# Refitted task durations in the list scheduler of a windowed attention and softplus feed-forward kernel

## Chip, cores and metric

One core of a Trainium2 chip. The metric is the device time of one execution in microseconds, the median of three runs.

## The reference

Windowed attention over 8 batches, 8 heads, 576 positions and 64 columns per head, then a feed-forward part with softplus on the 4608 tokens it gives. All in float32.

```python
scores = scale * np.matmul(q, k.transpose(0, 1, 3, 2))
mask_plain = (rel >= 0) & (rel < 32)                        # heads 0 to 3
mask_dil = (rel >= 0) & (rel < 128) & (rel % 4 == 0)        # heads 4 to 7
scores = np.where(masks, scores, -1e9)
attn = np.exp(scores - np.max(scores, axis=-1, keepdims=True))
attn = attn / (np.sum(attn, axis=-1, keepdims=True) + 1e-09)
x = np.matmul(attn, v)            # then 4608 tokens x 512
h = x @ w_in                      # 512 x 2048
g = np.maximum(h, 0.0) + np.log1p(np.exp(-np.abs(h)))
out = g @ w_out                   # 2048 x 512
```

## The kernel before, in words

The 4608 tokens are 9 chunks of 512. Attention of a chunk is 4 groups, one for each pair of heads, so there are 36 groups, `groups[0]` to `groups[35]`. For a group TensorE makes two visits, both of small matmuls: the scores (64 of them, `score_of`, tile `sv_ps<-k,q`) and, later, the values (64 of them, `value_of`, tile `sv_ps<-pt,v`). Between the two lies a chain: VectorE scales and masks the scores (L441) and takes the maximum (L452), ScalarE computes 8 exponentials (L463), VectorE the divisor (L475, L478), the division (L481) and a transpose of 32 x 32 squares (L503), and two DMAs through DRAM turn the squares (`turned`, then `pt`). The values of group n - 1 and the scores of group n use the two halves of the same banks.

The feed-forward part works on weights and activations that are split into a high and a low part, so a product is three wide matmuls (128 x 128 by 128 x 512). Chunks 0 to 2 go in 48 slots (`h_part`, `o_part`, softplus in between). Chunks 3 to 8 go as three doubles of two chunks; each double multiplies 2 x 2 blocks by seven products in place of eight: `product` (tiles `h_x`, `h_y`) for `w_in`, with an `aside` that takes every product out of its bank (L1424 on ScalarE, L1426 on VectorE), a late softplus unit of three ScalarE operations (L1437, L1440, L1443) and one VectorE operation (L1447) on 128 x 1024, sums of blocks (L1462), a high part on ScalarE and a low part on VectorE (L1467, L1471), and then `block_step` (tile `o_ps`) for `w_out`.

Two things order the work. Up to slot 22 (`HANDED`) the order is a written list (`OPENING`) and a loop that spreads VectorE's work over the slots. After that a list scheduler plans the rest: each piece of work is a `Task` with an engine, a cost in microseconds, tasks that it depends on, and a rank. The scheduler runs a clock; when an engine is free in the plan it emits the open task of the lowest rank on VectorE, ScalarE, GpSimd (POOL) and SyncE (SP, which issues the DMAs), and for TensorE chooses between three queues: `first` (h and products), `second` (o and block steps) and `visits`. Emission order is the order on each engine's queue on the chip; nothing is reordered there, and each instruction waits for the semaphores of what it needs. So a planned time has no force on the chip: only the order has.

`Task.open` is the test of whether a task may begin, `run` books an engine's time and the task's end, `values_of` and `attention` make the tasks of attention. `choose` takes the scores of group n when they are open and `joins` says that the values of group n - 1 can go with them (then both are emitted as one visit), or when they are overdue, or when neither other queue is open. `joins` asks that the turned squares landed at least `MARGIN` ago in the plan. At least 8 us (`VISIT_EVERY`) pass between visits. DMAs have a planned rate and landing time, `RATE` and `LANDING`.

Of the kernel before, what the change touches and what calls it, by code (L numbers as in the profile page):

```python
# [66 lines left out]
VALUED = 14.6, 17.1, 19.8  # L67
URGENT = -20.0
HANDED_VISIT = 2.0
MARGIN = 0.4  # L70
VISIT_EVERY = 8.0
NEG = -1.0e9
DEPTH = 4
# [43 lines left out]
def tile_windowed_attention_softplus_ffn(  # L117
# [804 lines left out]
    def score_of(n):  # L922
        shared[n] = two_banks("sv_ps")
        groups[n].score(shared[n])
# [91 lines left out]
    assert not events  # L1016

    MM, LATENCY, RATE, LANDING = 0.227, 0.06, 0.32, 2.3
    SHARED, FROM_PSUM = 1.0, ("aside", "put", "scaled", "max", "turn", "resumed", "finished", "plus 2", "plus 3", "plus 4")
    DVE, ACT, POOL, SP, PE = "DVE", "ACT", "POOL", "SP", "PE"  # L1020
    steps = (
# [9 lines left out]
    class Ring:  # L1031
# [7 lines left out]
        def take(self, until):  # L1039
            self.holders = self.holders[1:] + [until]  # L1040

    class Task:

        serial = itertools.count()
# [13 lines left out]
        def open(self, t):  # L1058
            return (
                self.after <= t + 1e-9  # L1060
                and all(
                    d.over(t + LATENCY * (getattr(d, "engine", PE) == self.engine != PE)) for d in self.deps
                )
                and all(ring.open(t) for ring, _ in self.takes)
                and (self.engine != SP or self.rank < 2.0 or arrived[0] <= t)
            )
# [28 lines left out]
    free_at = dict.fromkeys((PE, *queues), 0.0)  # L1095
# [8 lines left out]
    def run(task, t, engine=PE):  # L1104
        for ring, until in task.takes:
            ring.take(until)
        task.emit()
        cost = task.cost
        if engine == DVE and cost > 0.40 and not task.name.startswith(FROM_PSUM):
            cost += min(max(free_at[POOL] - t, 0.0), SHARED)  # L1110
        if task.engine == SP:
            free_at[SP] = t + 0.08
            task.end = arrival(t, task.cost)
        else:
            free_at[task.engine] = t + cost
            task.end = t + cost + LATENCY + 0.2 * (task.engine == PE)
        heapq.heappush(ends, task.end)
        heapq.heappush(ends, free_at[task.engine])
        if engine in queues:
            queues[engine].remove(task)  # L1120
# [172 lines left out]
    def values_of(n):  # L1293

        deps = [brought.get(n), loaded.get((n, "v")), scaled_of.get(n + 1), x_done.get(n - 1)]
        v = valued[n] = Task(f"values {n}", PE, 1.30, lambda: value_of(n), deps)
        if n + 1 < len(groups):
            loaded[n + 1, "v"] = Task(f"v {n + 1}", SP, 0.512, groups[n + 1].load_v, [v], rank=1.0)
        x_done[n] = Task(
            f"x {n}", ACT, 0.60, groups[n].x_high, [v, scaled_of.get(n + 1), *x_uses.get(n // 2, [])], rank=0.3  # L1300
        )

    def attention(n):

        soon[0] = SOONER
        if n == len(groups):
            values_of(n - 1)
            return
        g = groups[n]
        deps = [scaled_of.get(n - 1), x_done.get(n - 2), loaded[n, "k"], loaded[n, "q"]]  # L1310
        s = scored[n] = Task(f"scores {n}", PE, 1.06, lambda: score_of(n), deps)
        scaled = scaled_of[n] = Task(
            f"scaled {n}", DVE, 0.69, g.maximum, [s, turned_of.get(n - 1), masks_in.get(g.c)], rank=0.25
        )
        last = Task(f"max {n}", DVE, 0.69, g.greatest, [scaled], rank=0.26)
        loads(n + 1)
        values_of(n - 1)
        for t in range(NB):
            last = Task(
                f"exps {n} {t}", ACT, 0.34, lambda t=t: g.exponentials(slice(t, t + 1)), [last], rank=0.3 + 0.01 * t  # L1320
            )
        last = Task(f"divisor {n}", DVE, 0.40, g.divisor, [last], rank=0.3)
        last = Task(f"divide {n}", DVE, 0.70, lambda: g.divide(nc.vector), [last], rank=0.3)
        last = turned_of[n] = Task(f"turn {n}", DVE, 0.71, g.turn_squares, [last, sent_squares.get(n - 1)], rank=0.3)
        last = sent_squares[n] = Task(f"send {n}", SP, 0.256, g.send_squares, [last], rank=0.1)
        brought[n] = Task(f"bring {n}", SP, 0.5, g.fetch_squares, [last, valued[n - 1]], rank=0.1)
# [203 lines left out]
    for d in range(DOUBLES):  # L1530
        for p in range(NPAIR):
            for k, (x, weights, role, begins, to, temp) in enumerate(steps):
                b = (role + p) % 2
                task = Task(
                    f"product {d} {p} {k}", PE, 6 * MM,
                    lambda d=d, p=p, w=weights, x=x, b=b, s=begins: product(d, p, w, x, b, s),
                )
                n = len(steps) * p + k
                base = given + 2 * len(in_turn) * d
                if d == 0:  # L1540
                    task.upto = min(base, given - 2 * NKT + n)
                else:
                    task.upto = base - SPILL + min(n, SPILL)
                task.upto += due(d, n)
                product_done[d, p, x] = product_done[d, p, weights] = task
                at_n = len(steps) * (NPAIR * d + p) + k
                task.deps.append(asides.get(at_n - 2) or plus_done[46 + k])
                first.append(task)
                c = p // 2
                if isinstance(to, int):  # L1550
                    emit = lambda to=to, b=b, temp=temp: aside(temps(to), b, temp)
                else:
                    emit = lambda p=p, to=to, b=b, temp=temp: aside(raw_g(p // 2, *to)[:, p % 2], b, temp)
                mine = asides[at_n] = Task(
                    f"aside {d} {p} {k}", ACT if temp is None else DVE, 0.62 if temp is None else 0.70,
                    emit, [task, before],
                )
                before = mine
                if isinstance(to, int):
                    if d == 0 and p == 0:  # L1560
                        mine.deps.append(Later(lambda: written.get(NPAIR - 1)))
                    continue
                if d and p % 2 == 0:
                    users = {(0, 0): "s2", (0, 1): "s4", (1, 0): "s3", (1, 1): "s1"}
                    mine.deps.append(block_done[d - 1, users[to], c])
                    if to == (1, 1):
                        mine.deps.append(combined[d - 1, "s2", c])
                    if to == (0, 0):
                        mine.deps.append(combined[d - 1, "s4", c])
                elif d == 0 and p % 2 == 0:  # L1570
                    tag = 4 * c - 3 + {(0, 0): 0, (1, 1): 1, (1, 0): 2, (0, 1): 3}[to]
                    if c or to == (0, 1):
                        if tag % 2 == 0 or tag // 2 < RESIDENT:
                            mine.deps += [product_done[0, tag // 2, w] for w in (("b21",), ("b22", "t4"))[tag % 2]]
                        mine.deps.append(
                            Later(lambda q=tag // 2: two_kept.get(q)) if tag % 2 else kept_one[tag // 2]
                        )
                    else:
                        mine.deps.append(out_free[16 + tag])
                if p % 2 == 0:  # L1580
                    unit_first[to] = mine
                    continue
                key = c, *to
                name = f"{d} {key}"
                n = softened
                softened += 1
                plus = unit_done[d, key] = Task(f"plus {name}", DVE, 1.24, lambda key=key: late_softplus(key))
                takes = [(e_ring, plus)]
                one = Task(f"abs {name}", ACT, 1.16, lambda n=n, key=key: abs_of(n, key), [mine, unit_first[to], last_abs[0]], takes=takes)
                last_abs[0] = one  # L1590
                two = Task(f"exp {name}", ACT, 1.16, lambda key=key: late_exp(key), [one])
                plus.deps.append(Task(f"log {name}", ACT, 1.16, lambda key=key: late_log(key), [two]))
                if n == 1:
                    one.deps.append(Later(lambda: two_kept.get(6)))
        for turn, (i, c) in enumerate(in_turn):
# [167 lines left out]
    for n in range(double, len(groups)):  # L1763

        def both(n=n):
            score_of(n)
            value_of(n - 1)

        together[scored[n]] = Task(f"both {n}", PE, 2.10, both)
    spaced, done_second = HANDED_VISIT, 0  # L1770

    def joins(v, t):
# [219 lines left out]
```

## Time and profile before

| what | us |
|---|---|
| median of 3 runs | 831.25 (829.7 to 832.61) |
| the profiled execution's own time | 833.33 |
| its span, first to last instruction | 831.5 |
| TensorE busy | 815.6 |
| VectorE busy | 656.1 |
| ScalarE busy | 577.7 |
| GpSimd busy | 64.0 |

The granted TensorE clock was 0.989 over the span, and 1.00 in every slice after the first 50 us. A busy TensorE is not TensorE at its pace: matmuls are pipelined and their ends are modelled, so the starts of groups of matmuls are what to compare. In the rows below PE is TensorE, PEld its weight load, DVE VectorE, ACT ScalarE, POOL GpSimd and SP SyncE; L12 is line 12 of the kernel, and `out<-in` are the program's tile names.

### The profile page before, as it was taken

What the parts mean: (1) busy time and instruction counts of PE and PEld (TensorE: products, weight loads), DVE (VectorE), ACT (ScalarE), POOL (GpSimd) and SP (SyncE); (2) the same over time, 40 slices, a digit from 0 to 9 for tenths busy, and PEclk for the clock granted to TensorE, in tenths of its full rate; (3) what the DMA queues carried; (4) which work ended last, traced back from release to release, by engine and by line L of the source; (5) the groups of instructions that cost most, each with busy time, mean ns of one, the idle gap of its engine ahead of it and who ended that gap; (6) DMA issues with size and microseconds to landing.
All of it is one profiled execution on the core that took longest, in us unless ns stands there. A gap on an engine that the chain in (4) does not pass through costs nothing.

```text
span 831.5 us, 19565 instructions
## 1 busy us (share of the span) xinstructions
PE 815.6 (98%) x7841; PEld 662.6 (80%) x7841; DVE 656.1 (79%) x935; ACT 577.7 (69%) x1241; POOL 64.0 (8%) x74
## 2 busy tenths in 40 slices
PE   6899999999999999999999999999999999999997
PEld 3688888888888888788888888788878888888786
DVE  5798899957897798678889986778798957577964
ACT  6797778857676877578889546786796436776632
POOL 0000000031353360000000000000000000000000
PEclk7899999999999999999999999999999999999999
DMA  8788944468999887665777769897867576667662
GB/s 249 249 273 267 308 132 144 135 205 264 300 318 340 308 317 236 208 201 187 219 228 238 259 198 309 271 279 255 269 222 235 175 242 215 185 194 215 215 200 105
DMA packets 99947, 194.82 MB, mean 234 GB/s; under 512 B 10128, under 2 KB 43024, under 8 KB 99856
## 3 DMA queue, kind: packets, MB, share of 16 engines
q1 hardware_dynamic: 99712, 193.29, 72.1%
q8 instruction: 62, 1.02, 0.5%
q10 hardware_dynamic: 144, 0.28, 0.1%
q14 instruction: 29, 0.24, 0.1%
HBM read 145.29 MB, written 48.23 MB: 233 GB/s over the span
## 4 chain that ended last, share of the span: by engine, by line
PE 92%; DMA 4%; DVE 1%; ACT 1%; issue 0%; SPq 0%; ACTq 0%
PE o_ps L238 41%; PE h_ps L238 16%; PE h_x L238 14%; PE h_y L238 13%; PE sv_ps L238 6%; DMA q<-qp 1%; PE a_ps L238 1%; DMA t<-w_o 1%; DMA turned<-squares 1%; DMA raw<-w 1%; DMA consts<-cst 1%; PE s_ps L238 0%; PE t_ps L492 0%; DVE g L1471 0%; DMA k<-kpl 0%
## 5 line engine op out<-in xcount | busy, mean ns | idle before, releaser
L238 PE MATMUL o_ps<-g,t 128*128 128x512 f32 x864 | 209.6, 390 | 1.5 <-DMA t<-w_o 1.1
L238 PEld LDWEIGHTS o_ps<-g,t 128*128 128x128 f32 x864 | 161.3, 188 | 36.5 <-DMA t<-w_o 1.5
L238 PE MATMUL o_ps<-g,parts 128*128 128x512 f32 x576 | 142.1, 392 | 0.0
L238 PE MATMUL h_ps<-xh,parts 128*128 128x512 f32 x384 | 130.9, 397 | 0.0
L238 PEld LDWEIGHTS o_ps<-g,parts 128*128 128x128 f32 x576 | 107.1, 188 | 22.4
L1467 ACT CAST g<-stored 128x1024 fp32r<-128x1024 f32 x72 | 75.6, 1050 | 66.8 <-PE o_ps L238 64.9
L1471 DVE TENSOR_TENSOR g<-stored,g 128x1024 fp32r<-128x1024 f32 x72 | 87.8, 1221 | 32.4 <-ACT g L1467 32.2
L238 PEld LDWEIGHTS h_ps<-xh,parts 128*128 128x128 f32 x384 | 72.7, 189 | 15.5
L463 ACT ACTIVATE s<-s,nm 128x64 f32<-128x64 f32 x224 | 74.8, 337 | 12.1 <-DVE nm L452 11.7
L238 PE MATMUL h_ps<-xl,parts 128*128 128x512 f32 x192 | 75.3, 392 | 0.0
L238 PE MATMUL h_x<-s,t 128*128 128x512 f32 x276 | 70.6, 391 | 0.0
L238 PE MATMUL h_y<-s,t 128*128 128x512 f32 x276 | 70.6, 391 | 0.0
L799 POOL TENSOR_TENSOR a<-a 128x256 f32<-128x256 f32 x64 | 58.0, 914 | 99.8 <-DVE a L794 87.7
L1447 DVE SCALAR_TENSOR_TENSOR stored<-stored,e 128x1024 f32<-128x1024 f32 x48 | 58.4, 1219 | 4.4 <-ACT e L1443 4.4
L238 PEld LDWEIGHTS h_x<-s,t 128*128 128x128 f32 x276 | 51.5, 188 | 10.9
L238 PEld LDWEIGHTS h_y<-s,t 128*128 128x128 f32 x276 | 51.5, 188 | 10.8
L1462 DVE TENSOR_TENSOR stored<-stored 128x1024 f32<-128x1024 f32 x48 | 58.3, 1221 | 0.5
L1443 ACT ACTIVATE e<-e 128x1024 f32<-128x1024 f32 x48 | 50.8, 1060 | 1.1
L1440 ACT ACTIVATE e<-e 128x1024 f32<-128x1024 f32 x48 | 50.8, 1058 | 0.8
L1437 ACT ACTIVATE e<-stored 128x1024 f32<-128x1024 f32 x48 | 50.4, 1055 | 1.2 <-DVE stored L1426 0.7
L669 DVE SCALAR_TENSOR_TENSOR e<-h_ps,e 128x512 f32<-128x512 f32 x48 | 32.8, 683 | 21.7 <-ACT e L1147 16.9
L675 ACT CAST g<-e 128x512 fp32r<-128x512 f32 x48 | 29.5, 618 | 18.5 <-DVE e L669 9.6
(104 smaller groups left out, 1257.7 us busy)
## 6 DMA issues: line engine op xcount, KB each, us to landing
t<-w_o SPq DMA_DIRECT2D x84, 512.0 KB, 4.2
raw<-w SPq DMA_DIRECT2D x64, 256.0 KB, 4.3
v<-vp SPq DMA_DIRECT2D x28, 512.0 KB, 5.1
t<-w SPq DMA_DIRECT2D x20, 512.0 KB, 4.3
t<-w_two SPq DMA_DIRECT2D x20, 512.0 KB, 4.1
q<-qp SPq DMA_DIRECT2D x35, 256.0 KB, 3.9
w_o<-stage SPq DMA_DIRECT2D x32, 256.0 KB, 4.7
t<-w_one SPq DMA_DIRECT2D x16, 512.0 KB, 4.8
```

Source lines behind the costliest of these rows:

```text
L238: return tc.keep_in_program_order(nc.tensor.matmul(**kw))
L463: pin(nc.scalar.activation(out=self.blocks[:, t], in_=src, func=AF.Exp, bias=self.nm[:, t : t + 1], scale=1.0 / 8.0 if self.masked else 1. ...
L669: pin(nc.vector.scalar_tensor_tensor(out=e, in0=tiles.pop(i), scalar=0.0, in1=e, op0=ALU.max, op1=ALU.add))
L675: pin((copy or nc.scalar.copy)(out=gh, in_=ready[i]))
L799: pin(nc.gpsimd.tensor_tensor(out=out, in0=in0, in1=in1, op=ALU.subtract))
L1437: pin(nc.scalar.activation(out=es[key], in_=raw_g(*key), func=AF.Abs))
L1440: pin(nc.scalar.activation(out=es[key], in_=es[key], func=AF.Exp, scale=-1.0))
L1443: pin(nc.scalar.activation(out=es[key], in_=es[key], func=AF.Ln, bias=1.0))
L1447: pin(nc.vector.scalar_tensor_tensor(out=h, in0=h, scalar=0.0, in1=es.pop(key), op0=ALU.max, op1=ALU.add))
L1462: pin(nc.vector.tensor_tensor(out=raw_g(c, *PLACE[name]), in0=raw_g(c, *PLACE[a]), in1=raw_g(c, *PLACE[b]), op=op))
L1467: pin(nc.scalar.copy(out=set_of(k)[0], in_=raw_g(c, *PLACE[name])))
L1471: pin(nc.vector.tensor_tensor(out=low, in0=raw_g(c, *PLACE[name]), in1=high.bitcast(F32), op=ALU.subtract))
```

## The change

New costs for some tasks; an engine of the plan (VectorE, ScalarE) is free 0.10 us before the end of its task, 0.01 us for the exponentials; a task may depend on one that the same engine still has under way by that much; `MARGIN` doubles. Nothing else differs.

```diff
-MARGIN = 0.4
+MARGIN = 0.8
...
     MM, LATENCY, RATE, LANDING = 0.227, 0.06, 0.32, 2.3
+    OVERLAP, EXP_OVERLAP = {"DVE": 0.10, "ACT": 0.10}, 0.01
...
+    def overlap_of(task):
+        if not isinstance(task, Task):
+            return 0.0
+        return EXP_OVERLAP if task.name.startswith("exps") else OVERLAP.get(task.engine, 0.0)
+
...
                 and all(
-                    d.over(t + LATENCY * (getattr(d, "engine", PE) == self.engine != PE)) for d in self.deps
+                    d.over(t + (LATENCY + overlap_of(d)) * (getattr(d, "engine", PE) == self.engine != PE))
+                    for d in self.deps
                 )
...
-            free_at[task.engine] = t + cost
+            free_at[task.engine] = t + cost - overlap_of(task)
             task.end = t + cost + LATENCY + 0.2 * (task.engine == PE)
...
-        v = valued[n] = Task(f"values {n}", PE, 1.30, lambda: value_of(n), deps)
+        v = valued[n] = Task(f"values {n}", PE, 1.20, lambda: value_of(n), deps)
...
-        s = scored[n] = Task(f"scores {n}", PE, 1.06, lambda: score_of(n), deps)
+        s = scored[n] = Task(f"scores {n}", PE, 0.93, lambda: score_of(n), deps)
...
-                one = Task(f"abs {name}", ACT, 1.16, ...
+                one = Task(f"abs {name}", ACT, 1.07, ...
-                two = Task(f"exp {name}", ACT, 1.16, lambda key=key: late_exp(key), [one])
-                plus.deps.append(Task(f"log {name}", ACT, 1.16, lambda key=key: late_log(key), [two]))
+                two = Task(f"exp {name}", ACT, 1.07, lambda key=key: late_exp(key), [one])
+                plus.deps.append(Task(f"log {name}", ACT, 1.07, lambda key=key: late_log(key), [two]))
...
-        together[scored[n]] = Task(f"both {n}", PE, 2.10, both)
+        together[scored[n]] = Task(f"both {n}", PE, 1.99, both)
```

## Rows read from the trace of the kernel before

**Rows 1.** The page's first part: busy us (share of the span) xinstructions.

```profile
PE 815.6 (98%) x7841; PEld 662.6 (80%) x7841; DVE 656.1 (79%) x935; ACT 577.7 (69%) x1241; POOL 64.0 (8%) x74
```

**Rows 2.** Stages: us, busy us (xinstructions) of PE PEld DVE ACT POOL, PEclk, DMA share, GB/s.

```profile
0.00:167.60 167.60, 158.38 (x2049) 124.37 (x2050) 140.38 (x278) 131.80 (x372) 5.92 (x10) 0.95 0.68 218
167.60:637.00 469.40, 467.36 (x4959) 381.94 (x4958) 377.00 (x509) 341.41 (x756) 58.04 (x64) 1.00 0.80 257
637.00:827.00 190.00, 189.56 (x836) 156.30 (x834) 137.66 (x150) 104.49 (x114) 0.00 (x0) 1.00 0.61 195
```

**Rows 3.** Tile `sv_ps` on PE from 165 to 831 us, and its waits.

```profile
L238 PE MATMUL sv_ps<-pt,v x1600: 211/219/241, 168.7 to 635.6; 64*64 64x32 f32 x178
L238 PE MATMUL sv_ps<-k,q x1536: 212/216/240, 167.9 to 609.7; 64*32 64x64 f32 x192
...
  DMA pt<-turned: 1.0, 2
```

**Rows 4.** Chain of waits over the span: start us, us, what (the longest pieces).

```profile
173.51 2.72 PE h_ps L238 x12
...
529.70 6.12 DMA t<-w_o
610.61 5.78 DMA turned<-squares
```

**Rows 5.** Timeline of PE around a shared visit: start us, us, what.

```profile
570.78 1.52 PE L238 MATMUL h_x<-s,t 128*128 128x512 f32 x6
...
575.58 1.54 PE L238 MATMUL h_x<-a,t 128*128 128x512 f32 x6
```

**Rows 6.** Timeline of PE around scores alone and values alone.

```profile
388.59 1.52 PE L238 MATMUL h_y<-s,t 128*128 128x512 f32 x6
...
392.32 1.52 PE L238 MATMUL h_y<-a,t 128*128 128x512 f32 x6
393.68 1.52 PE L238 MATMUL o_ps<-g,t 128*128 128x512 f32 x6
...
397.69 1.52 PE L238 MATMUL h_y<-a,parts 128*128 128x512 f32 x6
```

**Rows 7.** Timeline of PE at waits of the planned stage.

```profile
535.86 1.66 PE L238 MATMUL o_ps<-g,t 128*128 128x512 f32 x6 [1.06 <-DMA t<-w_o]
...
619.78 1.12 PE L238 MATMUL sv_ps<-pt,v 64*64 64x32 f32 x60 [0.62 <-DMA pt<-turned]
...
775.60 2.79 PE L238 MATMUL o_ps<-g,t 128*128 128x512 f32 x11 [0.45 <-DVE g L1471]
```

**Rows 8.** Timeline of DVE: two operations, the second independent of the first.

```profile
419.02 0.69 DVE L1426 TENSOR_TENSOR stored<-h_x,a 128x512 f32<-128x512 f32 x1
419.63 0.68 DVE L481 TENSOR_TENSOR s<-s,ri 128x512 f32<-128x512 f32 x1
```

**Rows 9.** Timeline of DVE: two operations, the second reads what the first writes.

```profile
609.15 0.69 DVE L481 TENSOR_TENSOR s<-s,ri 128x512 f32<-128x512 f32 x1
609.87 0.71 DVE L503 STREAM_TRANSPOSE squares<-s 128x512 f32<-128x512 f32 x1
```

**Rows 10.** Timeline of ACT: the second depends on the first, the third on neither.

```profile
428.89 1.06 ACT L1440 ACTIVATE e<-e 128x1024 f32<-128x1024 f32 x1
429.99 1.06 ACT L1443 ACTIVATE e<-e 128x1024 f32<-128x1024 f32 x1
430.95 1.03 ACT L349 CAST a<-x_full 128x1024 fp32r<-128x1024 f32 x1
```

**Rows 11.** Timeline of ACT: exponentials 7 and 8 of the last visit.

```profile
602.53 0.19 ACT L463 ACTIVATION_READ_ACCUMULATOR s<-s,nm 128x1 f32 x1
603.13 1.06 ACT L1437 ACTIVATE e<-stored 128x1024 f32<-128x1024 f32 x1 [0.41 <-DVE stored L1426]
...
607.44 0.34 ACT L463 ACTIVATE s<-s,nm 128x64 f32<-128x64 f32 x1
```

**Rows 12.** The page's groups: one of the late softplus units' three ScalarE operations.

```profile
L1440 ACT ACTIVATE e<-e 128x1024 f32<-128x1024 f32 x48 | 50.8, 1058 | 0.8
```

More of the change, by code (lines that the diff above doesn't have):

```diff
@@ L1588, in tile_windowed_attention_softplus_ffn @@
                 takes = [(e_ring, plus)]
-                one = Task(f"abs {name}", ACT, 1.16, lambda n=n, key=key: abs_of(n, key), [mine, unit_first[to], last_abs[0]], takes=takes)
+                one = Task(f"abs {name}", ACT, 1.07, lambda n=n, key=key: abs_of(n, key), [mine, unit_first[to], last_abs[0]], takes=takes)
                 last_abs[0] = one
-                two = Task(f"exp {name}", ACT, 1.16, lambda key=key: late_exp(key), [one])
-                plus.deps.append(Task(f"log {name}", ACT, 1.16, lambda key=key: late_log(key), [two]))
+                two = Task(f"exp {name}", ACT, 1.07, lambda key=key: late_exp(key), [one])
+                plus.deps.append(Task(f"log {name}", ACT, 1.07, lambda key=key: late_log(key), [two]))
                 if n == 1:
```

## The prediction

> **What bounds the kernel now.** I read the page's first part, then a table of stages, then the planned stage closely. TensorE is busy for 815.6 of 831.5 us, VectorE for 79% and ScalarE for 69% of the span [rows 1]. The stages [rows 2] split at 167.60 us, where the planner's first visit begins, at 637 us, where attention is over, and at 827 us, where the matrix work is. Before 167.60 us the order comes from a written list and a pacing loop that the diff does not touch: 9.2 us without TensorE work lie there and stay. From 167.60 to 827 us, 659.4 us, TensorE has work for all but some 2.5 us, so little is left to win; but a busy row does not say that it ran at its pace, so I count the work.
>
> The stretch holds 4959 + 836 = 5795 matmuls [rows 2], of which 1536 + 1600 belong to visits of attention [rows 3]; 2659 wide ones (512 columns) remain. Twelve of these take 2.72 us in the chain of waits [rows 4], 0.2267 us each: 602.8 us. A visit costs TensorE more than its own matmuls, since the wide matmul on each side of it is slowed as well, so I take it from the start of the wide group before it to the start of the second group after it, less 12 wide matmuls. A shared visit: 575.58 - 570.78 - 2.72 = 2.08 us [rows 5]. Scores alone: 392.32 - 388.59 - 2.72 = 1.01; values alone: 397.69 - 393.68 - 2.72 = 1.29 [rows 6]. Sharing therefore saves 1.01 + 1.29 - 2.08 = 0.22 us. The timeline has 16 shared visits, 8 pairs that stayed apart, and the last values alone: 33.3 + 18.4 + 1.3 = 53.0 us.
>
> Work is 602.8 + 53.0 = 655.8 us, so stalls make 659.4 - 655.8 = 3.6 us. Three are seen [rows 7]: 1.06 us before 535.86 us, for weights that needed 6.12 us to land [rows 4]; 1.0 us in two waits [rows 3], the second before 619.78 us, for squares on their way for 5.78 us [rows 4] and the fetch behind them; 0.45 us before 775.60 us, for VectorE's low part of an operand. The rest is crumbs and restarts after these.
>
> **The change, part by part.** No instruction is added or removed. Only the planner's arithmetic changes, and with it the order on each queue, DMA issues included, after the hand-over at slot 22. What can change is 3.6 us of stalls and 8 x 0.22 = 1.8 us of visits apart: 5.4 us at the very best. What can be added has no such limit.
>
> *VectorE free 0.10 us sooner.* Two operations that do not depend on each other start 419.63 - 419.02 = 0.61 us apart though one lasts 0.69 [rows 8]. The old plan kept the engine for 0.69, the new one for 0.59: right for this case. With a dependence the next starts 609.87 - 609.15 = 0.72 us later [rows 9], and here the changed test of a task's dependences gives the overlap away too: it lets a task on the same engine begin at 0.59.
>
> *ScalarE the same, and 1.16 to 1.07 for three operations of each late softplus.* Independent: 430.95 - 429.99 = 0.96 us; dependent: 429.99 - 428.89 = 1.10 [rows 10]. The plan goes from 1.16 for both to 0.97 for both: 0.20 too much becomes 0.01 too much in the first case, and 0.06 too much becomes 0.13 too little in the second. The exponentials' 0.01 changes next to nothing.
>
> On the Trainium skill's page "VectorE: DVE Perf Modes", section "The DRAIN you can't avoid", the next operation does not start until the pipe of the one before is empty. By that rule the overlap would be false for all 659 VectorE instructions of the stage [rows 2], 659 x 0.10 = 66 us of its time costed away, and the sum would be the slower rival's, below; the row of 0.61 us shows otherwise for independent ones, the row of 0.72 us agrees for dependent ones.
>
> *What it gives.* The two engines stand 21 and 31% idle over the span [rows 1], so a plan that has them faster does not by itself make them so; it moves what is queued ahead of what. The last visit shows what that is worth: an exponential that ended at 602.72 us was followed by the next only at 607.44 [rows 11], with other work put between them, a softplus unit first, and the squares that TensorE missed before 619.78 us left later by that. A better order may cure this one and the 0.45 us at 775.60, with the next operand, queued right behind, late next. The 6.12 us of landing are a matter of DMA, whose figures in the plan stay: I leave it. Bounds for all stalls: none (-3.6) to twice as many (+3.6). I take a gain of 0.7, nearer to nothing, since a new order draws new stalls at other places.
>
> *Visits at 0.93, 1.20 and 1.99 instead of 1.06, 1.30 and 2.10.* Measured are 1.01, 1.29 and 2.08: the old figures were right to 0.05, the new ones are short by some 0.09. The plan then runs ahead by 16 x 0.09 + 8 x 0.17 + 0.09 = 2.9 us over the stage. TensorE does not go faster for that; the others get 0.09 us more per visit than planned. Cost: nothing; it is covered by their idle time, and with that gone a DMA timed to the clock would come early, which costs nothing either.
>
> *Margin 0.4 to 0.8.* The values join the scores only when their squares landed 0.8 us ago in the plan. The only waits for squares under a visit are the 1.0 us, in 2 waits [rows 3], both in a visit that stood apart, which the margin does not rule. So there is nothing to win, and some visits come 0.4 us later or stay apart. Against that a faster chain (maximum, exponentials, division, squares) in the plan brings the values sooner. Bounds: all 8 pairs join (-1.8) to 8 more come apart (+1.8). I take three fewer apart, 5 of 24: -0.7 us.
>
> Sum: -0.7 - 0.7 = -1.4 us against the profiled execution, 833.33 us (span 831.5 and 1.8 around it). That one stood 2.1 us above the median of the runs, 831.25; the forecast is 831.25 - 1.4 = 829.9 us.
>
> **The rivals.** *Faster: the stalls go.* If planned and real durations agree, the scores no longer go out alone because the plan had nothing else ready; two thirds of 5.4 us come back: -3.6, 827.7 us. For it: the visits apart come close together, three pairs one behind the other, as if the plan starved where the chip does not. Against it: the largest stall is a landing.
>
> *Slower: dependent operations are now costed too short.* There are 48 late softplus units [rows 12], each with two such steps on ScalarE: 2 x 0.13 = 0.26 us, 12.5 us in all. In slack stretches this vanishes; where ScalarE is planned full, high parts come late, VectorE's low parts behind them, and TensorE stands at the first matmul of a block. A third of it on the path would be +4.2 us, less 0.7 for visits: +3.5, 834.8 us. It decides from the point at which more than a quarter of it shows. For it: the old surplus was the cover for just this, and TensorE already waited 0.45 us for a low part. Against it: other work is often put between the steps, and ScalarE is 69% busy. By the rule of the Trainium skill's page "VectorE: DVE Perf Modes" all VectorE tasks would be in this rival too; as the 0.61 us contradicts it, it adds no more than 0.02 to the chance.
>
> *It does nothing:* the order hardly moves where it matters, 831.3 us. This lies inside the forecast's band.
>
> **How the numbers follow.** About 0.3%, 2.5 us, is what a measurement of this kernel can tell from no change. The forecast, with the do-nothing case in it, gets 0.52: most of 5.4 us would have to come back to be seen. Faster gets 0.28, slower 0.20 (0.18 and the 0.02). The range runs from just beyond the faster case, 827.0, to the slower one, 834.8.
>
> **What would show it.** Right: the same work in the planned stage, its length 1 to 2 us shorter than 659.4, about 5 pairs apart, one or two stalls of about 1 us at new places, VectorE's and ScalarE's busy time unchanged. The faster case would show 3 pairs apart or fewer and no single wait of TensorE over 0.5 us. The slower one would show waits of TensorE for VectorE's low parts in stretches with ScalarE busy nearly throughout. A stage before 167.6 us of another length would make the comparison void. The prediction is wrong if stalls in the planned stage fall below 1 us or rise above 6 us.

## The result, and the profile after

The changed kernel is slower by 0.6%: 838.31 us, the median of six runs, against 833.29 us for six of the kernel before, a ratio of 1.0063 with a 95% interval of 1.0041 to 1.0085. The profiled executions stand at 837.49 and 833.33 us. The forecast was 1.4 us faster; what came is 5.0 us slower, past the slower rival. The forecast was reckoned from the median of three runs, 831.25 us; six runs of the same kernel give 833.29, so 2.0 of the 8.4 us between the forecast and the measured time are the kernel before itself.

Table of stages of the changed kernel (columns as in [rows 2]):

```profile
0.00:167.60 167.60, 158.64 (x2048) 124.44 (x2050) 141.07 (x279) 131.74 (x372) 6.48 (x11) 0.95 0.68 216
167.60:640.00 472.40, 470.31 (x4970) 383.61 (x4970) 379.08 (x516) 345.22 (x762) 62.60 (x64) 1.00 0.78 256
640.00:831.00 191.00, 188.47 (x823) 153.41 (x822) 130.97 (x141) 99.31 (x108) 0.00 (x0) 1.00 0.61 193
```

The first 167.6 us are as before (158.64 us of TensorE work, 158.38 before). All of the loss lies in the planned stage. In what follows that stage runs from the first matmul of the first planned visit to the start of the last matmul, which gives 659.0 us for the kernel before (the prediction's 659.4 had other ends, and of its 2659 wide matmuls two lie before the visit and two were counted in both stretches) and 663.6 us for the changed one. Its work is 2655 wide matmuls at 0.2267 us and the visits at the prediction's three prices; what remains is called stalls, and it holds the waits, the slower restart behind each and crumbs. The kernel before: 654.9 of work, 4.2 of stalls. The changed one: 653.5 and 10.1. Work fell because sharing did what it should: the timeline shows 22 shared visits and 2 pairs apart, where there were 16 and 8. Stalls rose by 5.9 us.

Waits of TensorE in the changed kernel from 167 to 832 us: who waited for whom, us in total, times, the longest:

```profile
PE o_ps L238 <- DVE g L1478: 2.4, 5, 0.6
PE o_ps L238 <- DMA t<-w_o: 1.1, 2, 0.5
PE h_y L238 <- DVE a L1433: 0.7, 1, 0.7
PE h_x L238 <- DVE a L1433: 0.2, 1, 0.2
```

The same view of the kernel before:

```profile
PE o_ps L238 <- DMA t<-w_o: 1.1, 1, 1.1
PE sv_ps L238 <- DMA pt<-turned: 1.0, 2, 0.6
PE o_ps L238 <- DVE g L1471: 0.4, 1, 0.4
```

The wait for squares is gone, that for weights stays at 1.1 us, and five waits for a low part of an operand (L1478, L1471 before the change) stand where one stood; two more are for an `aside` that has to empty a bank. The waits in these lists are 4.4 of the 10.1 us of stalls, and were 2.5 of the 4.2. So two thirds of the rise lie in what the lists leave out: waits too short for them, and late starts behind a wait (the one of 0.74 us below costs 0.91). What each of the two adds is left open. Timeline of PE and then of DVE in the changed kernel around the longest stall:

```profile
698.69 1.52 PE L238 MATMUL h_x<-s,t 128*128 128x512 f32 x6
700.96 1.43 PE L238 MATMUL h_y<-a,t 128*128 128x512 f32 x5 [0.74 <-DVE a L1433]
```

```profile
697.95 1.22 DVE L1478 TENSOR_TENSOR g<-stored,g 128x1024 fp32r<-128x1024 f32 x1
699.08 1.22 DVE L1454 SCALAR_TENSOR_TENSOR stored<-stored,e 128x1024 f32<-128x1024 f32 x1
700.22 0.69 DVE L1433 TENSOR_TENSOR a<-h_y,temps 128x512 f32<-128x512 f32 x1
```

VectorE does not idle here. It began a softplus of 1.22 us (L1454) at 699.08, and the `aside` (L1433) that TensorE stood for had to wait behind it. TensorE's groups of six start 2.27 us apart in place of 1.36: 0.91 us lost to the order of two operations.

### The profile page after: what moved, and what is told of

The parts are those of the page before. It is cut to its first block, busy times and chain, and to the rows that moved or that the text cites. A ratio compares the mean times of both kernels' runs of the same rounds, so it can differ in the third digit from the quotient of the medians.

```text
span 835.7 us, 19549 instructions
## 1 busy us (share of the span) xinstructions
PE 818.0 (98%) x7839; PEld 661.6 (79%) x7841; DVE 652.5 (78%) x935; ACT 576.3 (69%) x1241; POOL 69.1 (8%) x74
## 4 chain that ended last, share of the span: by engine, by line
PE 76%; DMA 10%; ACT 6%; DVE 5%; issue 1%; SPq 1%; ACTq 0%; DVEq 0%
PE o_ps L238 36%; PE h_ps L238 13%; PE h_y L238 11%; PE h_x L238 11%; PE sv_ps L238 5%; DMA raw<-w 4%; DMA v<-vp 2%; DVE g L1478 1%; ACT e L1444 1%; DMA t<-w_o 1%; DMA q<-qp 1%; ACT e L1447 1%; DMA k<-kpl 1%; DVE stored L1454 1%; ACT e L1450 1%
## 5 line engine op out<-in xcount | busy, mean ns | idle before, releaser
L1478 DVE TENSOR_TENSOR g<-stored,g 128x1024 fp32r<-128x1024 f32 x72 | 87.9, 1220 | 39.2 <-ACT g L1474 39.1
L1454 DVE SCALAR_TENSOR_TENSOR stored<-stored,e 128x1024 f32<-128x1024 f32 x48 | 58.5, 1221 | 16.4 <-ACT e L1450 16.4
L799 POOL TENSOR_TENSOR a<-a 128x256 f32<-128x256 f32 x64 | 63.2, 994 | 95.4 <-DVE a L794 85.8
L669 DVE SCALAR_TENSOR_TENSOR e<-h_ps,e 128x512 f32<-128x512 f32 x48 | 32.8, 684 | 15.0 <-ACT e L1154 10.5
```

Of the source, the lines that this page charges most:

```text
L669: pin(nc.vector.scalar_tensor_tensor(out=e, in0=tiles.pop(i), scalar=0.0, in1=e, op0=ALU.max, op1=ALU.add))
L799: pin(nc.gpsimd.tensor_tensor(out=out, in0=in0, in1=in1, op=ALU.subtract))
L1454: pin(nc.vector.scalar_tensor_tensor(out=h, in0=h, scalar=0.0, in1=es.pop(key), op0=ALU.max, op1=ALU.add))
L1478: pin(nc.vector.tensor_tensor(out=low, in0=raw_g(c, *PLACE[name]), in1=high.bitcast(F32), op=ALU.subtract))
```

## The experiments

Four theories were tested. M: the margin. D: the new durations as such, above all dependent operations of one engine, which the changed test lets in 0.10 us early. R: any change of the plan draws its stalls anew, and the old plan was a lucky draw. O: long operations of VectorE or ScalarE stand ahead of short ones that TensorE needs.

**Dependent operations booked from the end of the one they follow.**

```diff
+    BEHIND = 0.03
...
-            free_at[task.engine] = t + cost - overlap_of(task)
-            task.end = t + cost + LATENCY + 0.2 * (task.engine == PE)
+            begun = max([t, *(d.end - LATENCY + BEHIND for d in task.deps
+                              if isinstance(d, Task) and d.engine == task.engine != PE)])
+            free_at[task.engine] = begun + cost - overlap_of(task)
+            task.end = begun + cost + LATENCY + 0.2 * (task.engine == PE)
```

> The changed kernel, but an operation that depends on one of its own engine is booked to begin 0.03 us after that one's end, as measured, in place of 0.10 us before it. Theory D (dependent operations are costed too short, so high and low parts come late): most of the new stalls go; the planned stage falls from 663.6 to 659 to 661 us, ratio to before 0.995 to 1.002. Theory M (the margin): no change, ratio 1.005 to 1.008. Theory R (any new plan draws its stalls anew, and the one before was a lucky draw): a ratio of 1.003 to 1.01, with stalls of 5 to 10 us at other places.

Measured: 835.19 us, ratio 1.005 (1.0032 to 1.0069); planned stage 660.3 us, 6.1 of them stalls. The stage fits D, the ratio lies above D's band. Theory R's band holds the ratio and the stalls too. One draw, so it decides nothing alone.

**TensorE's order written out as in the kernel before.** The planner's choice for TensorE is replaced by a string of letters, one for each task (first queue, second queue, a visit alone, a shared visit); it waits until the named task is open in the plan. Everything else is planned with the changed durations.

```diff
     def choose(t):
-        if visits and visits[0] in scores:
...
+        letter = written_order[0]
+        queue = {"1": first, "2": second}.get(letter, visits)
+        if not queue[0].open(t):
+            return None
```

> TensorE's order is written out as in the kernel before (16 shared visits, 8 pairs apart); VectorE, ScalarE and the DMAs are planned around it with the changed durations. Theory D, with the order of VectorE and ScalarE at fault: stalls stay, ratio 1.004 to 1.012. If TensorE's own order is at fault (it asks for blocks sooner than they can be ready): the stalls go, ratio 0.997 to 1.002. Theory M says the same as the second, since the margin only acts through TensorE's order.

Measured: 842.25 us, ratio 1.0134 (1.0107 to 1.0161), stage 668.9 us with 14.1 of stalls. TensorE asks for the same things in the same sequence as before and stalls three times as long. So the loss does not need TensorE's order, nor its shared visits: the order of VectorE, ScalarE and the DMAs alone can make it. The ratio lies somewhat above D's band.

The same with the start of dependent operations corrected as above:

> TensorE's order as in the kernel before, the others planned with the changed durations, and an operation that depends on one of its own engine begins 0.03 us after that one's end. Beside the run with the same TensorE order and the changed start of dependent operations (ratio 1.0134, 14.1 us of stalls). Theory D: most of the loss goes, ratio 0.998 to 1.004, stalls of 4 to 7 us. Theory R: it stays anywhere from 1.005 to 1.015.

Measured: 838.51 us, ratio 1.0105 (1.0086 to 1.0125), stage 664.7 us with 9.8 of stalls. Beside the run without the correction 4.2 us are gone, beside the kernel before 5.7 to 7.4 stay. D's bands, 0.998 to 1.004 and stalls of 4 to 7 us, are missed, and the ratio lies in R's: the correction may be a part of the loss, it is not all of it.

**The visits' old costs, and the old margin, each alone in the changed kernel.**

```diff
-        v = valued[n] = Task(f"values {n}", PE, 1.20, lambda: value_of(n), deps)
+        v = valued[n] = Task(f"values {n}", PE, 1.30, lambda: value_of(n), deps)
...
-        s = scored[n] = Task(f"scores {n}", PE, 0.93, lambda: score_of(n), deps)
+        s = scored[n] = Task(f"scores {n}", PE, 1.06, lambda: score_of(n), deps)
...
-        together[scored[n]] = Task(f"both {n}", PE, 1.99, both)
+        together[scored[n]] = Task(f"both {n}", PE, 2.10, both)
```

> The changed kernel with the visits' old costs 1.06, 1.30 and 2.10. If the plan runs ahead because visits are costed 0.09 us short, TensorE no longer reaches blocks too early: ratio 0.997 to 1.003. Theory D and M: little changes, 1.004 to 1.008. Theory R: anything from 1.000 to 1.010.

```diff
-MARGIN = 0.8
+MARGIN = 0.4
```

> The changed kernel with the old margin of 0.4. Theory M: the ratio falls to 0.997 to 1.003, with as many or more visits shared. Theory D: the stalls for low parts stay, 1.004 to 1.009; theory R: anything from 1.000 to 1.010.

Measured with the old visit costs: 837.48 us, ratio 1.008 (1.0058 to 1.0102), stage 664.2 us, stalls 10.5. As the changed kernel, at the upper end of D's and M's band: in this draw the visits' old costs give nothing back. With the old margin: 847.46 us, ratio 1.0196 (1.017 to 1.0222), stage 672.6 us, stalls 18.4, 19 shared visits. M's band is missed: the loss does not go with the wider margin, it grows, and fewer visits are shared, not more (22 in the changed kernel). One draw, here too, and its largest stall is a row to keep. PE's timeline, then the stages around it:

```profile
572.06 1.11 PE L238 MATMUL sv_ps<-pt,v 64*64 64x32 f32 x58
575.26 0.31 PE L238 MATMUL sv_ps<-pt,v 64*64 64x32 f32 x6 [2.08 <-issue]
575.50 2.93 PE L238 MATMUL h_y<-a,t 128*128 128x512 f32 x6
578.23 1.86 PE L238 MATMUL h_x<-s,t 128*128 128x512 f32 x6
579.93 1.53 PE L238 MATMUL o_ps<-g,t 128*128 128x512 f32 x6
```

```profile
560.00:572.00 12.00, 12.00 (x114) 9.55 (x112) 8.94 (x13) 8.33 (x19) 0.00 (x0) 1.00 0.71 241
575.40:579.00 3.60, 3.60 (x15) 2.85 (x11) 2.51 (x3) 1.12 (x3) 0.00 (x0) 0.53 0.55 165
579.00:590.00 11.00, 11.00 (x50) 9.12 (x49) 7.14 (x11) 10.91 (x26) 0.00 (x0) 1.00 0.65 201
```

Inside a shared visit TensorE stood for 2.08 us (for no operation that the profile names), and behind it the granted clock was 0.53 over 3.6 us, nearly all of it at 1.2 GHz: the next six wide matmuls took 578.23 - 575.50 = 2.73 us in place of 1.36, and the six behind them 579.93 - 578.23 = 1.70. The wait costs some 1.6 us more than itself.

**The same orders once more, and draws that mean nothing.** Second traces of both kernels say how far one order repeats. Then each was planned anew with a number that has nothing to do with the change: the planned landing time of a transfer.

> The kernel before, unchanged, for a second trace of it: how far do two executions of one order differ in the planned stage? All theories: 657.5 to 660 us there, stalls of 3 to 5 us at the same places; what differs in the whole lies in the first 168 us.

> The changed kernel, unchanged, for a second trace of it. All theories: 662 to 665 us in the planned stage, stalls of 9 to 11 us at the same places.

```diff
-    MM, LATENCY, RATE, LANDING = 0.227, 0.06, 0.32, 2.3
+    MM, LATENCY, RATE, LANDING = 0.227, 0.06, 0.32, 2.35
```

> The kernel before with one number moved that has nothing to do with the change: a transfer is planned to land after 2.35 us in place of 2.30. Theory R (every new plan draws its stalls anew, the old one was a lucky draw): a ratio of 1.004 to 1.015. Theories D and M: nothing that they name has changed, so 0.997 to 1.003.

> The kernel before with 2.25 us, its third draw. Theory D: 657 to 662 us in the planned stage. Theory R: 657 to 668.

> The changed kernel planned anew by a number that has nothing to do with the change: transfers land after 2.25 us in the plan. The planned stage of the changed kernel took 663.6 and 663.8 us. Theory D (the new durations as such cost time): 662 to 672 us again, above both draws of the old durations (657.3 to 659.0 and 660.7). Theory R (luck of the draw alone): anything from 657 to 668 us, so as likely below 661 as above.

> The same with 2.35 us. Theory D: 662 to 672 us in the planned stage; theory R: 657 to 668.

> The kernel of the run with dependent operations booked from the end of the one they follow (660.3 us in the planned stage), planned anew with a landing of 2.35 us. If dependent operations costed too short are what the new durations lose by: 659 to 664 us, as with the old durations (658, 660.7 and 661.3). If that run was a lucky draw: 664 to 669, as with the new ones (663.7, 666.7 and 668.1).

> The same with 2.25 us, and the same numbers: 659 to 664 us in the planned stage if it is the dependent operations, 664 to 669 if the first was luck.

> The changed kernel with an overlap of nothing on any engine; the new visits, softplus costs and margin stay. If the loss comes with the overlap (its part for dependent operations or the surplus that it takes away): 658 to 662 us in the planned stage. If it comes with the visits, the softplus costs or the margin: 664 to 669.

> The same with a landing of 2.35 us, a second draw: 658 to 662 us in the planned stage if it is the overlap, 664 to 669 if it is one of the others.

The last two set both overlaps to nothing (`{"DVE": 0.0, "ACT": 0.0}, 0.0`). Planned stage in us, stalls in brackets, by the landing time in the plan:

| durations | 2.25 | 2.30 | 2.35 |
|---|---|---|---|
| old | 661.3 (7.1) | 659.0 (4.2), 657.3 (2.5) | 660.7 (6.2) |
| changed | 666.7 (13.2) * | 663.6 (10.1), 663.8 (10.2) | 668.1 (14.3) * |
| changed, dependent operations from the end | 670.0 (15.8) * | 660.3 (6.1) | 661.5 (6.6) |
| changed, no overlap | | 662.9 (8.5) | 665.2 (10.4) * |

A star marks a trace in which TensorE's clock fell to half in the middle of the stage, behind a long wait, as in the rows above (once, in the last one twice); some 1.6 us a time are in its stalls for that. The whole times beside it: the second traces took 831.13 (before) and 837.61 us (changed), the first landing control has a ratio of 1.0051 (1.0035 to 1.0068), the others are single executions of 833.82, 842.19, 841.79, 834.5, 842.93, 834.61 and 839.41 us, in the order of the expectations from the kernel before with 2.25 us on.

Against the expectations: the second trace of the kernel before lies a little below its band, and one of its waits is missing; that of the changed kernel lies within. The first control came as R said, outside the band of D and M. The other draws of the old and the changed durations fit both D and R (668.1 us is just past R's end). With dependent operations corrected, 661.5 us is D's and 670.0 lies beyond both bands. Without overlap, 662.9 us lies between the two bands and 665.2 in the one for the other parts of the change.

Not every wait here is a matter of VectorE's or ScalarE's order. In seven traces TensorE stands once, for 0.37 to 2.09 us, among the small matmuls of a visit's values, with no operation that releases it. Among them are both nudged plans of the old durations (0.95 us with 2.35, 1.36 with 2.25), the changed one with 2.25 us, and the old margin above. The changed one's line of waits, and the line of its page on the DMA queue q8:

```profile
PE sv_ps L238 <- issue: 2.1, 1, 2.1
q8 instruction: 62, 1.02, 0.5%
```

The span holds 62 packets of instructions on that queue, and in all seven traces the latest of them had landed 1.2 to 1.5 us before TensorE went on. This points to a wait for code; no run tests it.

What follows. R is half right: 0.05 us on a number that concerns nothing costs the kernel before 0.5%, nearly as much as the change. But no draw of the changed durations lies below any of the old ones: 663.6 and more against 661.3 and less, three each. By luck alone three against three would fall so once in twenty times, and the three runs with one part put back (old visit costs 664.2, old margin 672.6, TensorE's old order 668.9 us) lie above as well. So the durations very likely have a cost of their own: 2.3 us between the nearest two, 6 between the means. Which part of them it is stays open; the softplus costs were never moved alone. Two of three draws with dependent operations corrected come down to the old ones, the third is the slowest of the table (4 us of it are a wait of 2.47 us for a DMA, `k<-kpl`, and the half clock behind it); the two without overlap lie between. Two or three draws with a spread of 2 to 10 us do not settle it.

**Single operations put in another place.** TensorE's and the DMAs' order is that of the changed kernel, to the last instruction; named operations wait, in the plan alone, for one that TensorE will need. First four:

```diff
+    for late, soon_one in (
+        ("plus 2 (0, 1, 0)", "aside 2 2 3"), ("abs 2 (3, 0, 1)", "high 2 a22 3"),
+        ("exp 2 (3, 1, 0)", "high 2 a12 1"), ("s4 2 0", "low 2 a12 1"),
+    ):
+        named[late].deps.append(named[soon_one])
```

> The changed kernel's own order, TensorE's and the DMAs' to the last instruction, with four operations of VectorE and ScalarE put behind one that TensorE waits for soon; 19 of 635 places on VectorE and 6 of 677 on ScalarE differ. Theory O (what is lost is single long operations that sit ahead of short urgent ones): the stalls at 699.8, 775.6 and 779.0 us (0.90, 0.51 and 0.57 us) go or shrink, 1.6 us with the restarts behind them, so 661.5 to 662.5 us in the planned stage in place of 663.7, and a ratio of 1.002 to 1.006. If the engines are simply too full there: the stalls only move, 663 to 664.5 us.

Measured: stage 661.9 us, stalls 8.3, as theory O had it; the ratio is 1.0056 (1.0038 to 1.0073), within O's band and not told apart from the changed kernel's by timing alone. The trace shows it: timeline of DVE, then of PE, where the 0.91 us were lost.

```profile
697.10 1.22 DVE L1488 TENSOR_TENSOR g<-stored,g 128x1024 fp32r<-128x1024 f32 x1
698.23 0.69 DVE L1443 TENSOR_TENSOR a<-h_y,temps 128x512 f32<-128x512 f32 x1
698.83 1.22 DVE L1464 SCALAR_TENSOR_TENSOR stored<-stored,e 128x1024 f32<-128x1024 f32 x1
```

```profile
697.86 1.52 PE L248 MATMUL h_x<-s,t 128*128 128x512 f32 x6
699.22 1.52 PE L248 MATMUL h_y<-a,t 128*128 128x512 f32 x6
700.70 1.66 PE L248 MATMUL h_x<-s,t 128*128 128x512 f32 x6
```

The `aside` (now L1443) comes before the softplus (L1464), and TensorE's groups start 1.36 us apart; 0.13 and 0.18 us come back as small waits behind it. In the last stretch of `w_out`, timeline of PE in the changed kernel and then with the four swaps:

```profile
769.95 6.04 PE L238 MATMUL o_ps<-g,t 128*128 128x512 f32 x24 [0.49 <-DVE g L1478]
776.35 3.06 PE L238 MATMUL o_ps<-g,t 128*128 128x512 f32 x12 [0.35 <-DVE g L1478]
779.81 2.83 PE L238 MATMUL o_ps<-g,t 128*128 128x512 f32 x11 [0.41 <-DVE g L1478]
```

```profile
768.48 5.79 PE L248 MATMUL o_ps<-g,t 128*128 128x512 f32 x24 [0.48 <-DVE g L1488]
774.66 5.51 PE L248 MATMUL o_ps<-g,t 128*128 128x512 f32 x23 [0.39 <-DVE g L1488]
780.00 2.88 PE L248 MATMUL o_ps<-s,t 128*128 128x512 f32 x12
```

One of three waits is gone. Three further swaps hold back the exponential of one softplus unit, the last step of another, and the last of the exponentials of a group of attention:

```diff
+        ("exp 2 (3, 0, 1)", "high 2 a12 0"), ("plus 2 (2, 1, 1)", "aside 2 6 3"),
+        ("exps 22 7", "abs 0 (0, 0, 0)"),
```

> The same with three more swaps, at the stalls near 350, 617 and 740 us or where the plan shows waits. Theory O: a further 0.5 to 1.0 us, 660.5 to 662 us in the planned stage, ratio 1.001 to 1.005. If the engines are too full: 663 to 664.5 us.

Measured: stage 660.9 us, stalls 7.4, ratio 1.0041 (1.0025 to 1.0056). In the last stretch one wait of 0.45 us is left, before 767.66 us, and TensorE then runs 47 matmuls without a break:

```profile
767.66 10.95 PE L248 MATMUL o_ps<-g,t 128*128 128x512 f32 x47 [0.45 <-DVE g L1488]
```

Seven operations in another place, with no duration changed on the chip, give back 663.7 - 660.9 = 2.8 us of the stage (663.7 is the mean of the changed kernel's two traces). The waits that were named shrink or go: that is theory O shown for these places, from one trace each; the timed ratios of this run and of the changed kernel overlap. The 7.4 us of stalls that are left still lie above the 2.5 and 4.2 of the kernel before.

**A draw that was looked for.** Measured visit costs, dependent operations booked 0.10 us after the end, and ten constants of the planner drawn anew (the expectation says nine):

```diff
+    BEHIND = 0.1
-DUE = 25
-APART = 3.5
+DUE = 23
+APART = 4.5
...
-MARGIN = 0.8
-VISIT_EVERY = 8.0
+MARGIN = 0.7
+VISIT_EVERY = 12.0
```

(and `BUSY` 1.06, `SPILL` 12, `SOONER` 16, `FAMILY_SOONER` 8, `LATE_VISITS` 15, `HANDED_VISIT` 0)

> The changed kernel with visits at the measured 1.01, 1.29 and 2.08 us, a dependent operation booked 0.10 us after the end of the one it follows, and nine of the planner's constants drawn anew, chosen for few planned waits under the measured durations. If what matters is a plan that knows the dependences and a good draw: 655.5 to 658.5 us in the planned stage, stalls of 2 to 4 us, ratio 0.996 to 1.001. If the surplus of the old durations is needed as cover: 660 us and more, ratio above 1.003.

Measured: 830.76 us against 831.0, ratio 0.9999 (0.9983 to 1.0015). The first visit comes 9 wide matmuls sooner, so the stage of 658.9 us stands for 658.9 - 9 x 0.2267 = 656.8 on equal footing, with 2.2 us of stalls, the fewest of all (2.5 in the second trace of the kernel before), and a single wait in TensorE's list of waits from 167 to 832 us:

```profile
PE o_ps L238 <- DVE g L1481: 0.5, 1, 0.5
```

So durations close to the measured ones and few stalls can go together; as the constants were searched for, this one draw does not say which of the two did it, and the timed runs do not tell it from the kernel before. No version here beats it.

## Why the prediction was wrong, point by point

**The bound.** Not contradicted: the planned stage is TensorE's work plus stalls, and the first stage did not move. That 5.4 us was the most that could come back was not put to the test.

**Visits.** Right in mechanism, the term too small: 0.7 us for 5 pairs left apart; 2 were left, 6 x 0.22 = 1.3 us.

**Stalls.** This is the step that failed: "I take a gain of 0.7, nearer to nothing, since a new order draws new stalls at other places", between bounds of -3.6 and +3.6. It was +5.9 (4.2 to 10.1), or +7.8 against the second trace of before. I bounded the loss by the stalls that one trace showed, as if these were usual. They were low for this planner: nudged by 0.05 us of landing time, the old durations gave 6.2 and 7.1, already near the bound. (Of these, about 1.0 and 1.4 us are the waits with no operation named.) That the order of the kernel before was the best of three draws was not among the bounds. The prediction's own sign of being wrong, stalls above 6 us, came.

**The surplus.** The slower rival named the right side, at 834.8 us: 3.5 over the median it was reckoned from, with 4.2 more of stalls; 5.0 came, with 5.9. Its sign came too: waits for low parts, with ScalarE busy nearly throughout before them. Stages of the changed kernel ahead of four of the five (columns as in [rows 2]):

```profile
436.00:444.10 8.10, 7.53 (x35) 5.89 (x33) 8.06 (x10) 8.07 (x15) 0.00 (x0) 1.00 0.90 309
610.00:618.60 8.60, 8.03 (x155) 6.04 (x153) 8.56 (x10) 8.54 (x14) 0.00 (x0) 1.00 0.74 242
763.50:778.30 14.80, 13.96 (x59) 10.56 (x58) 11.52 (x12) 14.69 (x17) 0.00 (x0) 1.00 0.67 209
```

The sign does not decide it, since ScalarE was also busy for 13.86 of 14.60 us before the one such wait of the kernel before. The rival's mechanism, dependent operations costed 0.13 us too short on ScalarE, is supported by three pairs of runs, in which the correction (it covers VectorE too) took the stage from 663.7 to 660.3, from 668.1 to 661.5 and, with the old order of TensorE, from 668.9 to 664.7 us; it is contradicted by a fourth, 666.7 to 670.0. The places that were looked at show another form of it: VectorE or ScalarE begins a long operation in front of a short one that TensorE needs. By the rule of the Trainium skill's page "VectorE: DVE Perf Modes", section "The DRAIN you can't avoid", as the prediction took it, the overlap itself would be false. The same section of the Trainium skill's page goes on that a next operation that is not held starts earlier, which the prediction did not weigh; the changed kernel's rows agree with that for operations that do not depend on each other (a low part at 697.95, the next start at 699.08: 1.13 us for one that lasts 1.22).

**Margin.** "There is nothing to win" is not borne out: with the old margin the changed kernel took 672.6 us in the stage, not 663.7, of which some 3.7 us are the wait with no operation named and the half clock behind it. One draw, so the margin's share is open; the loss does not go when the margin is put back.

**Visit costs.** No cost was predicted, and the one draw with the old ones shows none: 664.2 us.

**The range** ended at 834.8, the slower rival's price: a third of 12.5 us, a share that no row gave. The stalls' bound of +3.6 beside it was a mirror of what could be won, and nothing in the kernel makes the two sides alike.

## What to carry to other kernels

Where a planner writes a static order, the change of any number in it can be a new draw, and a single comparison can measure the draw as much as the change. Run a control that moves a number without meaning, and two or three draws of each side, before a constant gets the credit or the blame.

A stall in such a kernel is best read at its place: which operation did the late engine begin instead, and who waited? A swap of two named operations with all other orders held fixed costs one run and answers it.

## What was not expected of the hardware

One order repeats closely: the changed kernel's stage took 663.6 and 663.8 us in two traces, and its stalls came back at the same places, the one just before 701 us with 0.90 and 0.89 us, three in the last stretch with the same 0.65, 0.51 and 0.57 us. The kernel before differs by 1.7 us, of which 1.4 are a wait for squares, a DMA, that its second trace does not have.

The first stage, whose order no version changes up to the first visit, adds to the uncertainty of the whole: the first planned visit began between 165.7 and 169.5 us in the traces here (165.0 in the last version, which has it sooner), nearly as much spread as the change's effect has size. Between the two traces of the kernel before it is the lesser part: 0.5 us there, 1.7 in the planned stage.

A wait of 2 us can cost nearly twice its length, since the clock falls behind it. In these traces, from 100 us to the last matmul, TensorE had eight waits of 1.59 to 2.47 us; behind seven of them its granted clock fell to 1.2 GHz, behind one of 1.79 us it did not, nor behind any of the shorter ones, the longest of them 1.36, 1.37, 1.41 and 1.55 us. None of the changed kernel's own waits, 0.74 us at most, was followed by it. Of the five slowest plans (672.6, 670.0, 668.9, 668.1 and 666.7 us) four had such a fall in the stage, the one of 668.9 us had none.
